# Every 16 MB of key and value loads, one 2 MB transfer issued as 112 partitions and two pieces of eight

## The chip, the cores and the metric

The kernel runs on one core of one Trainium2 chip. The metric is the device time of one execution in microseconds (us). Before the change the median of three runs was 1109.37 us (1105.71, 1109.37 and 1112.99).

## The reference, cut to what matters

One token for each of 8 batch rows passes through two identical layers. Each layer is an attention block over a cached sequence (16 query heads, 8 key/value heads, 4096 positions of 256 numbers) followed by an MLP block. Both layers read the same key cache and the same value cache.

```python
q = (x @ wq).reshape(B, Sq, Hq, Dh)                       # B=8, Sq=1, Hq=16, Dh=256
k = jnp.repeat(k_cache, 2, axis=1)                        # cache: 8 x 8 x 4096 x 256, bf16
scores = jnp.einsum("bhqd,bhkd->bhqk", q, k) * (Dh ** -0.5)
p = _softmax(scores, axis=-1)
o = jnp.einsum("bhqk,bhkd->bhqd", p, v)
...
x = x + _A_ref(_layernorm(x), A_k_cache, A_v_cache, A_wq, A_wo)    # attention
x = x + _B_ref(_layernorm(x), B_w1, B_w2, B_w3, B_w4)              # MLP
x = x + _A_ref(...)                                                # the same caches again
x = x + _B_ref(...)
```

Keys and values of one (batch row, head) are 2 MB each, so the two caches together hold 268 MB. All arithmetic hangs on streaming them through the core, once for each layer, less what is kept on the chip between the two.

## The kernel before, in words

**The cache buffer.** The tensor `kv` holds 30 slots ("quarters", `QUARTERS`) of 4 KB in each of the 128 partitions of SBUF. A (batch row, head) tile of K or V is viewed as 128 partitions of 16 KB of neighbouring positions and is cut along that row into four units of 4 KB per partition, 512 KB each; a unit takes one slot. K units are transposed by TensorE (`transpose_piece`, L1165), copied back over themselves by VectorE or ScalarE (`evacuate`, L1148 and L1149) and multiplied with the queries (L985); V units are used as they land (L1050). Some units of the first layer stay in their slots until the second layer has used them (`KEEP_K`, `KEEP_V`).

**The order of work.** The program is a list of operations with dependencies. `Plan.schedule` plays it through with assumed durations and writes down one fixed order for each engine. Loads go in program order on the SyncE queue (SP): `next_kv` (L191) waits in the plan until slots come free and merges up to four neighbouring units of one tile into one transfer of up to 2 MB (16 KB in each partition), and calls `issue_kv`. On the chip, a transfer that overwrites slots waits at SP for the instruction that used them last (a matmul of L985 or L1050); a consumer waits for the transfer's own semaphore, one for each slot (`slot_sem`), to reach the count that `issue_kv` has written into `o.dma`. `Plan.emit` (L446) turns this into waits and adds 16 to the semaphore with every transfer (L453 to L455).

**Weights.** `dma_once` and `dma` (L596 to L606) load each weight once, on the same queue. Two of them are loaded in halves that cover 64 partitions each: `wqx_sb` (L1236, 256 KB each) near the start, and `w3x_sb` (L1244, 112 KB each) later in the first batch row. The input `x_row` comes as two small transfers of eight rows; the output leaves in two transfers (L1193), the first of six rows of 896 bytes, the second of two.

**Batch rows.** Layer 1 of a row and layer 2 of the row before alternate; in each row there is a long stretch in which 2 MB transfers follow one another, and a shorter one around the MLP block in which loads are cut into 512 KB and 1 MB, because slots come free one at a time.

Of the kernel before, what the change touches and what calls it, by code (L numbers as in the profile page):

```python
# [6 lines left out]
P = 128  # L7
# [13 lines left out]
KEEP_K = 5  # L21
KEEP_V = 6
HOLD = 2
MARGIN4, MARGIN2 = 6, 2
REP = 24
AT = (-4, -3, -2)
# [433 lines left out]
def bass_interleave_layers__gqa_block_cached__mixer_s_mlp__decode_kernel(  # L460
# [119 lines left out]
    slot_sem = [nc.alloc_semaphore(f"s_slot{i}") for i in range(QUARTERS)]  # L580
    slot_n = [0] * QUARTERS
# [24 lines left out]
                4 * at - 0.5, *row)  # L606

    loads = [0]

    def issue_kv(o, n, q):  # L610

        (cache, b, h), u = o.unit.tile, o.unit.u
        src = cache[b, h].rearrange("(m s) d -> m (s d)", m=P)[:, u * 2048:(u + n) * 2048]
        dst = kv[:, q * 2048:(q + n) * 2048]
        slot_n[q] += 1
        o.emit = lambda eng: eng.dma_start(dst, src)  # L616
        o.dma = (slot_sem[q], 16 * slot_n[q])
        o.dur = ((n << 15) / 26.88e3 + 8 * 0.008) / FASTER

# [318 lines left out]

    KEPT_K[HKV - 1] = range(4 - HOLD)
    KEPT_V = {HKV - 1 - i: range(max(4 * i + 4 - KEEP_V, 0), 4) for i in range((KEEP_V + 3) // 4)}  # L940
    done = {}

    def front(layer, b, h, prio=None):
# [21 lines left out]
        for u in banks_of:  # L965

            ks[u] = ks[u + HOLD - 4]
            back_in[u + HOLD - 4] = u
        held = {}
# [462 lines left out]
```

## Time and profile before

| | |
|---|---|
| median of three runs | 1109.37 us |
| span of the profiled execution | 1109.5 us |
| TensorE busy | 971.3 us (88%) |
| VectorE, ScalarE, GpSimd busy | 573.0, 288.1, 97.9 us |
| bytes moved by DMA | 441.13 MB in 54099 packets |
| the SyncE queue's packets, share of 16 DMA engines | 96.9% |
| instruction fetch (queue 8) | 153 packets, 2.51 MB, 0.9% |
| transfers of 2 MB | 72 of K, 55 of V |
| chain of work that ended last | TensorE 54%, DMA 32%, SyncE queue 4% |

The profiled execution's own time is its span, 1109.5 us, 0.1 us from the median of the runs. A transfer is spread over 16 DMA engines; its packets are what the engines move one after another. "Share" counts the time that packets took as a share of 16 engines over the span, and where packets overlap by a few ns it comes out a little over 1. Windows below are in us from the start of the span.

### The profile page before, as it was taken

What the parts mean: (1) busy time and instruction counts of PE and PEld (TensorE: products, weight loads), DVE (VectorE), ACT (ScalarE), POOL (GpSimd) and SP (SyncE); (2) the same over time, 40 slices, a digit from 0 to 9 for tenths busy, and PEclk for the clock granted to TensorE, in tenths of its full rate; (3) what the DMA queues carried; (4) which work ended last, traced back from release to release, by engine and by line L of the source; (5) the groups of instructions that cost most, each with busy time, mean ns of one, the idle gap of its engine ahead of it and who ended that gap; (6) DMA issues with size and microseconds to landing.
All of it is one profiled execution on the core that took longest, in us unless ns stands there. A gap on an engine that the chain in (4) does not pass through costs nothing.

```text
span 1109.5 us, 42648 instructions
## 1 busy us (share of the span) xinstructions
PE 971.3 (88%) x19517; PEld 777.4 (70%) x19517; DVE 573.0 (52%) x1782; ACT 288.1 (26%) x844; POOL 97.9 (9%) x275
## 2 busy tenths in 40 slices
PE   4889889898889887999888898898889998899987
PEld 4678657786668756786667776777557886587774
DVE  4345445555455543655555554565445655366544
ACT  1133113331224301242122321234113330243120
POOL 0000010100100101010000100101010010101010
PEclk9899989989999969999898898999899997899898
DMA  9999999999999999999999989999999999999993
GB/s 332 410 424 421 389 388 424 425 421 380 412 424 424 418 344 428 422 425 418 378 424 423 421 326 381 425 424 420 387 402 424 425 410 364 420 423 407 329 399 163
DMA packets 54099, 441.13 MB, mean 398 GB/s; under 512 B 5776, under 2 KB 8992, under 8 KB 26528
## 3 DMA queue, kind: packets, MB, share of 16 engines
q1 hardware_dynamic: 53920, 438.41, 96.9%
q8 instruction: 153, 2.51, 0.9%
q14 instruction: 26, 0.21, 0.0%
HBM read 438.38 MB, written 0.01 MB: 395 GB/s over the span
## 4 chain that ended last, share of the span: by engine, by line
PE 54%; DMA 32%; SPq 4%; issue 4%; DVE 4%; ACT 1%; POOL 0%
PE psT L1165 20%; DMA kv<-in_A_k_cache_dram 20%; PE psM L985 15%; DMA kv<-in_A_v_cache_dram 12%; PE psP L1050 8%; SPq L616 4%; PE psR L1099 3%; PE psM L814 2%; PE psM L927 1%; PE psM L930 1%; DMA w3x_sb<-in_B_w_dram 1%; PE psP L1373 1%; PE psP L1074 1%; DVE oS L1066 1%; ACT pT L1019 1%
## 5 line engine op out<-in xcount | busy, mean ns | idle before, releaser
L1165 PE MATMUL psT<-ident_f,kv 128*128 128x128 f32 x2816 | 390.2, 284 | 23.3 <-DMA kv<-in_A_k_cache_dram 21.3
L1148 DVE COPY kv<-psT 128x512 f32<-128x512 f32 x415 | 284.3, 690 | 177.5 <-PE psT L1165 171.7
L1165 PEld LDWEIGHTS psT<-ident_f,kv 128*128 128x128 f32 x2816 | 313.2, 144 | 49.0 <-DMA kv<-in_A_k_cache_dram 28.3
L1149 ACT COPY kv<-psT 128x512 f32<-128x512 f32 x321 | 186.8, 586 | 385.4 <-PE psT L1165 384.9
L1050 PE MATMUL psP<-kv,pT 128*2 128x256 bf16 x4096 | 186.9, 292 | 27.8 <-issue 13.2
L985 PEld LDWEIGHTS psM<-q2T,kv 128*128 128x128 bf16 x4096 | 127.3, 99 | 48.0 <-issue 35.1
L985 PE MATMUL psM<-q2T,kv 128*128 128x48 bf16 x4096 | 142.5, 188 | 18.2 <-issue 14.4
L985 PEld LDWEIGHTS psM<-q1T,kv 128*128 128x128 bf16 x4096 | 135.1, 97 | 18.9 <-issue 12.5
L985 PE MATMUL psM<-q1T,kv 128*128 128x48 bf16 x4096 | 143.9, 184 | 2.2 <-issue 1.2
L1050 PEld LDWEIGHTS psP<-kv,pT 128*2 128x2 bf16 x4096 | 78.5, 84 | 70.2 <-issue 25.3
L1019 ACT ACTIVATE pT<-sS,nb,fac 128x32 bf16<-128x32 f32 x128 | 52.7, 417 | 244.0 <-DVE nb L1013 244.0
L1009 POOL PARTITION_ALL_REDUCE gm<-pm x128 | 45.6, 356 | 763.1 <-DVE pm L1007 718.0
L1004 DVE COPY sS<-psM 128x64 f32<-128x64 f32 x128 | 28.6, 223 | 108.4 <-PE psM L985 105.6
L1064 DVE CAST oS<-psP 128x256 bf16<-128x256 f32 x128 | 54.0, 422 | 49.3 <-PE psP L1050 46.9
L1099 PE MATMUL psR<-wo_sb,oT 128*1 128x448 bf16 x448 | 68.6, 390 | 4.2 <-DVE oT L1080 2.3
L1023 POOL PARTITION_ALL_REDUCE Db<-rs x128 | 51.1, 399 | 213.2 <-ACT pT L1019 213.2
L1074 PE MATMUL psP<-sel,oS 128*128 128x2 bf16 x512 | 32.1, 166 | 34.6 <-DVE oS L1066 31.1
L1074 PEld LDWEIGHTS psP<-sel,oS 128*128 128x128 bf16 x512 | 25.2, 99 | 52.5 <-DVE oS L1066 43.8
L1019 ACT ACTIVATE pT<-sS,nb 128x32 bf16<-128x32 f32 x128 | 40.9, 326 | 69.6 <-DVE nb L1013 69.5
L1066 DVE TENSOR_TENSOR oS<-psP,oS 128x256 bf16<-128x256 f32 x128 | 54.1, 423 | 3.5
L814 PEld LDWEIGHTS psM<-x2c,wq_sb 128*128 128x128 bf16 x768 | 30.5, 98 | 19.4 <-issue 6.9
L814 PE MATMUL psM<-x2c,wq_sb 128*128 128x24 bf16 x768 | 36.4, 184 | 6.2 <-issue 5.3
(157 smaller groups left out, 579.1 us busy)
## 6 DMA issues: line engine op xcount, KB each, us to landing
kv<-in_A_k_cache_dram SPq DMA_DIRECT2D x72, 2048.0 KB, 20.5
kv<-in_A_v_cache_dram SPq DMA_DIRECT2D x55, 2048.0 KB, 17.2
kv<-in_A_v_cache_dram SPq DMA_DIRECT2D x121, 512.0 KB, 7.5
kv<-in_A_v_cache_dram SPq DMA_DIRECT2D x54, 1024.0 KB, 10.6
kv<-in_A_k_cache_dram SPq DMA_DIRECT2D x23, 1024.0 KB, 12.6
kv<-in_A_v_cache_dram SPq DMA_DIRECT2D x5, 1536.0 KB, 10.9
kv<-in_A_k_cache_dram SPq DMA_DIRECT2D x12, 512.0 KB, 8.1
wo_sb<-in_A_wo_dram SPq DMA_DIRECT2D x1, 3584.0 KB, 45.4
```

The costliest lines, as they stand in the source:

```text
L814: last = t.matmul(bank[:, at + i * step:at + i * step + copies], w, r, start=(kc == 0), stop=(kc == 3))
L985: last = t.matmul(ps[:, SB + 2 * i:SB + 2 * i + 2 * REP], a[:, c:256:2], bcast(rhs(c), REP, 1), start=(c == 0), stop=(c == 1))
L1019: return a.activation(pT[nr][:, :, :].rearrange("p i j -> p j i")[:, jj, :], sview[:, jj, :], ACT.Exp, bias=nb[nm][:, jj:jj + 1], scale=sc ...
L1023: plan.op("pool", lambda gp: gp.partition_all_reduce(Db[nr][:, :], rs[nr][:, :], P, RO.add), 0.5, "sum", rd=[("rs", nr, 0), ("rs", nr, 1)] ...
L1050: last = t.matmul(ps[g4:g4 + 2, PV0:PV0 + DH], pT[nr][:, i, :], slot_ap(q, s * 256, 256), start=(i < 4), stop=(i >= 28), skip_group_check= ...
L1064: plan.op("dve", lambda v: v.tensor_copy(oS[:, 0, :], po), 0.36, "o", rd=[("pv", par, x) for x in range(4)], wr=["oS0"], banks=[bk], prio=hi)
L1066: plan.op("dve", lambda v: v.tensor_tensor(oS[:, 1, :], po, oS[:, 0, :], ALU.subtract), 0.36, "o", rd=["oS0"] + [("pv", par, x) for x in r ...
L1074: last = t.matmul(ps[:, PV1 + 2 * c:PV1 + 2 * c + 2], oS[:, w, c:DH:2], sel[:, :], start=(w == 0), stop=(w == 1))
L1099: last = t.matmul(psR[r:r + 1, 0:D], oT[no][:, i % 2, i // 2:i // 2 + 1], wo_sb[:, a:a + D], start=(k == 1 and i < 2), stop=(k == HKV - 1 ...
L1148: return e.tensor_copy(dst, psT[bank][:, :])
L1149: return e.copy(dst, psT[bank][:, :])
L1165: last = t.transpose(psT[bank][:, s * P:(s + 1) * P], src, ident_f[:, :])
```

## The change

`issue_kv` counts the units that it has issued. Whenever 32 units (16 MB) or more have gone out since the last time and the transfer at hand has four units (2 MB), this transfer is issued as three: one of the first 112 partitions and two of eight partitions each (112 to 119, 120 to 127). All three add 16 to the same slot's semaphore, and the count that consumers wait for grows by 48 instead of 16. The plan is computed with the same assumed duration, so the order on every engine stays as it was; the SyncE queue gets two more DMA instructions behind each such transfer. There are 21 of them, 9 of K and 12 of V.

```diff
+SPLIT, EVERY = 8, 32
...
     loads = [0]
+    since = [0]
 
     def issue_kv(o, n, q):
 
         (cache, b, h), u = o.unit.tile, o.unit.u
         src = cache[b, h].rearrange("(m s) d -> m (s d)", m=P)[:, u * 2048:(u + n) * 2048]
         dst = kv[:, q * 2048:(q + n) * 2048]
-        slot_n[q] += 1
-        o.emit = lambda eng: eng.dma_start(dst, src)
+        since[0] += n
+        top = P
+        if n == 4 and since[0] >= EVERY:
+            since[0] = 0
+            top = P - 16
+        slot_n[q] += 1 + (P - top) // SPLIT
+
+        def go(eng):
+            last = eng.dma_start(dst[0:top, :], src[0:top, :])
+            for p in range(top, P, SPLIT):
+                last.then_inc(slot_sem[q], 16)
+                last = eng.dma_start(dst[p:p + SPLIT, :], src[p:p + SPLIT, :])
+            return last
+        o.emit = go
         o.dma = (slot_sem[q], 16 * slot_n[q])
         o.dur = ((n << 15) / 26.88e3 + 8 * 0.008) / FASTER
```

## The prediction

> **What bounds the kernel now.** I read the page's first lines and its DMA rows, then the windows over single stretches, then the waits of SP. The page first:
>
> ```profile
> span 1109.5 us, 42648 instructions
> ...
> DMA  9999999999999999999999989999999999999993
> ...
> DMA packets 54099, 441.13 MB, mean 398 GB/s; under 512 B 5776, under 2 KB 8992, under 8 KB 26528
> ...
> q1 hardware_dynamic: 53920, 438.41, 96.9%
> q8 instruction: 153, 2.51, 0.9%
> ...
> kv<-in_A_k_cache_dram SPq DMA_DIRECT2D x72, 2048.0 KB, 20.5
> kv<-in_A_v_cache_dram SPq DMA_DIRECT2D x55, 2048.0 KB, 17.2
> ```
>
> The 16 DMA engines are at work for 96.9% of the span for SP's queue alone. A 2 MB transfer needs 2.097 MB / 423 GB/s = 4.96 us, but lands 20.5 us after its issue, so about four stand in line. The windows (us, PE, PEld, DVE, ACT, POOL busy, PE clock, DMA share, GB/s) tell long stretches from others:
>
> ```profile
> 20.60:26.60 6.00, 5.23 (x42) 4.14 (x39) 3.29 (x5) 2.93 (x5) 0.00 (x0) 1.00 1.05 272
> 30.00:40.00 10.00, 8.97 (x203) 7.42 (x202) 3.21 (x13) 2.37 (x10) 1.53 (x4) 0.83 1.00 422
> ...
> 114.00:122.00 8.00, 6.50 (x108) 4.08 (x103) 4.31 (x11) 1.31 (x5) 0.75 (x2) 1.00 1.06 353
> ...
> 145.00:245.00 100.00, 89.13 (x1708) 73.00 (x1705) 51.27 (x140) 29.44 (x86) 9.81 (x26) 0.93 1.01 420
> ...
> 385.00:415.00 30.00, 25.76 (x536) 16.09 (x536) 13.45 (x62) 1.98 (x10) 1.11 (x3) 0.72 0.95 351
> ...
> 550.00:635.00 85.00, 73.43 (x1417) 61.28 (x1415) 43.98 (x120) 24.27 (x73) 8.70 (x23) 0.92 1.01 425
> ```
>
> In the long stretches (145 to 245, 550 to 635) the engines are never idle and move 420 to 425 GB/s, while PE has 11% and 14% to spare: what a DMA engine loses there, the span loses. In the short ones (385 to 415) the share falls to 0.95. The first and third rows show something else: full engines (1.05, 1.06) that move only 272 and 353 GB/s. These are where the two transfers of `wqx_sb`, and later the two of `w3x_sb`, land, each covering 64 partitions:
>
> ```profile
> L599 SPq DMA_DIRECT2D wqx_sb<-in_A_wq_dram x2: 555/584/614, 4.2 to 4.8; - x2
> ...
> DMA to landing us min/median/max: 21.1/21.4/21.8
> ```
>
> (issued at 4.2 and 4.8 us, landed at 25.3 to 26.6).
>
> SP itself is no bound; it waits for PE to free slots:
>
> ```profile
> SPq L616 <- PE psM L985: 468.7, 86, 26.2
> SPq L616 <- PE psP L1050: 374.0, 151, 16.5
> ```
>
> **The change part by part.**
>
> *SP.* 21 transfers become three, 42 DMA instructions more. One takes 0.33 us at SP, 14 us in all, 0.65 us at a time. Queued behind them is the next transfer, for which PE waits only some 20 us later; SP waited 843 us in the two rows above. Cost 0; without four transfers in line it would be 14 us. The signals of the pieces are packets of 4 bytes, 9 ns each: 2 x 21 x 9 ns = 0.4 us, neglected.
>
> *How the rows fall.* The page counts 5776 packets under 512 B. That is 16 signals for each of 359 transfers (5744), 8 + 8 for the two of `x_row`, 6 + 2 for the outputs, and 8 data packets of 128 B. So 64 partitions still use 16 engines, and eight rows use eight, as the change says. A 16 KB row takes 4.96 / 8 = 0.62 us on its engine (0.614 in the packet records). A split gives eight engines 7 + 1 + 1 = 9 rows and the others 7: plus and minus 0.614 us, over 21 splits 12.9 us either way.
>
> *What it could balance.* In the packet records, the instruction fetches come in turn on the same eight engines: each takes 1.02 to 1.10 us, and the 16 KB packet behind it 1.08 to 1.16 instead of 0.614, so one costs some 1.55 us of its engine. 153 / 8 = 19 for each: 29.6 us more on these eight than on the others, 1.41 us between two splits, against the 1.23 us that a split shifts between the halves. If the fetching engines were all outside the pieces' eight, the change would even them out. I followed engines back to back (a packet starts 3 to 4 ns before the one ahead of it ends) from the six 896 B packets of the first output: five of these six engines never fetch, one does. If a transfer of six and one of eight start from the same engine, the pieces' eight hold at least one fetching engine, which then gets later: +12.9 us instead of -12.9. [...]
>
> *Transfers that cover fewer than 128 partitions.* This is the main term. The trace has no such transfer of 112 or of eight partitions among traffic; the nearest are those of 64.
> - Lowest price, by transfer: the window of `wqx_sb` lost (1 - 272/422) x 6 us = 2.13 us for two, that of `w3x_sb` (1 - 353/422) x 8 = 1.31 us for two, so 0.65 to 1.07 us each. Three at 0.65, plus the 0.61 us row: 2.6 us a split.
> - By packet: beside `wqx_sb`, 16 KB packets took some 1.13 us (1.08 to 1.18 mostly) instead of 0.614, and its own 4 KB packets 0.29 instead of 0.159. A transfer of 112 rows with 7 such packets on an engine loses 7 x 0.52 = 3.6 us, the two pieces cost 2 x 1.13 - 0.61 = 1.65 us: 5.3 us a split.
> - Highest: the slowest 16 KB packet in the records, 2.32 us, in the first microseconds of traffic, for the pieces (2 x 2.32 - 0.61 = 4.0), and 1.18 for the 112 rows (7 x 0.57 = 4.0): 8.0 us.
> - From below: the 896 B packets of `x_row`, eight partitions on an empty queue, mostly took 0.039 us, as elsewhere. Then there is no price at all, and the rows' -12.9 to +12.9 us remain.
>
> I take the price by packet, since the split's packets are of the size whose slowing was seen: 5.3 us. Eighteen of the 21 are issued in long stretches or at their edge; three (at 648, 778 and 1057 us of the old order) fall in short ones, where engines wait for slots, and are left out; without that cover they cost 16 us more. 18 x 5.3 = 95 us.
>
> [...]
>
> *What is late next.* Eight engines fall behind at every split; each transfer counts as landed when its last engine is done, so L1165 and L1050 wait, slots come free later, and the other eight engines run dry.
>
> *Sum.* 1109.5 + 95 = 1205 us. The 1109.5 are the profiled execution's own span; the median of the runs is 0.1 us lower.
>
> **Rivals.**
> - *Balance* (not slower): no price for fewer partitions, and all fetching engines outside the pieces' eight. At best -12.9 us, 1097; if the short stretches even out half of the lag anyway, 1103. For it: 1.41 us against 1.23 us. Against it: the two slow windows, and the one output engine that fetches.
> - *Wrong half*: no price, but one fetching engine or more among the eight: 1109.5 + 12.9 = 1122. For it: that engine; against it, the slow windows.
> - *Hidden*: the line of four transfers lets engines differ by several us, and the short stretches bring them together again: 1109.5. For it: share 0.95 there. Against it: 1.01 in the long ones, with no slack at the end of them.
> - That the pieces use all 16 engines, and nothing is shifted, is excluded by the 5776 small packets.
>
> **How the numbers follow.** A change of 1% (11 us) is about what a measurement of this kernel can tell from none; its three runs span 0.7%. The forecast has 0.72, balance 0.09, wrong half 0.08, hidden 0.11. The forecast's own range goes from 18 x 2.6 = 47 (1156) to 21 x 8.0 = 168 (1278). To hold 8 in 10 it reaches down over hidden, to 1106, and up to 1280; balance and the outermost of the forecast stay outside. Faster by over 1%: half of balance, 0.05. Within 1%: hidden, the other half, and a little of wrong half, 0.17. Slower: 0.78.
>
> **What would show it.** Small packets rise by 21 x 16 to 6112. In long windows the share stays at 1.0 or falls a little while the rate drops: a split for every 20.9 MB, 49.4 us before, takes 54.7, so 420 becomes some 380 GB/s. Waits of L1165 and L1050 for DMA grow, PE's busy time stays near 971 us. If the long windows still show 420 GB/s or more, the price is wrong, and the span then says which half fetches: below 1109, the others; above, the pieces' own.

## The result, and the profile after

The changed kernel takes 1288.74 us (median of four runs, 1280.30 to 1289.97) against 1111.18 us for the kernel before, run beside it: a ratio of 1.1599, 95% interval 1.1558 to 1.1639. The profiled execution's own span is 1286.2 us. The forecast was 1205 us, with a range from 1106 to 1280; the loss is 177.6 us where 95 were forecast. Over 21 splits it is 8.5 us each.

The page of the kernel after:

```profile
span 1286.2 us, 42690 instructions
...
PE 1025.5 (80%) x19517; PEld 812.3 (63%) x19517; DVE 574.5 (45%) x1782; ACT 287.8 (22%) x844; POOL 97.6 (8%) x275
...
DMA  9999999999999989999899998999999999999994
GB/s 347 372 348 320 375 314 402 334 307 342 347 403 327 366 250 334 398 299 380 263 341 413 320 358 273 344 416 329 345 349 323 371 339 366 410 329 418 339 319 191
DMA packets 54435, 441.13 MB, mean 343 GB/s; under 512 B 6112, under 2 KB 9328, under 8 KB 26864
...
q1 hardware_dynamic: 54256, 438.41, 96.6%
...
kv<-in_A_k_cache_dram SPq DMA_DIRECT2D x63, 2048.0 KB, 25.5
kv<-in_A_v_cache_dram SPq DMA_DIRECT2D x43, 2048.0 KB, 25.5
```

The engines are as busy as before (96.6% against 96.9%) and move the same bytes, but at 343 GB/s instead of 398. Busy share alone would show nothing wrong: a slow packet counts as busy. The small packets are 6112, as forecast (21 x 16 more): the split does what it says.

Windows of the kernel after (us, busy time of PE, PEld, DVE, ACT and POOL, PE clock, DMA share, GB/s), the first three around one split:

```profile
190.00:220.00 30.00, 27.89 (x490) 21.81 (x488) 15.11 (x40) 8.41 (x22) 2.26 (x6) 0.89 1.01 425
220.00:240.00 20.00, 12.17 (x162) 10.35 (x163) 7.08 (x18) 2.66 (x7) 0.75 (x2) 0.83 1.00 238
240.00:270.00 30.00, 27.60 (x487) 24.98 (x484) 17.70 (x44) 11.64 (x35) 3.77 (x10) 0.94 1.02 421
340.00:440.00 100.00, 81.02 (x1452) 68.36 (x1450) 47.13 (x122) 29.32 (x80) 8.28 (x22) 0.91 1.01 365
```

Between splits the old rate of 420 to 425 GB/s is back. Around the split, for 20 us, full engines (1.00) move 238 GB/s: (1 - 238/423) x 20 = 8.7 us are lost, the 8.5 us a split of the whole. TensorE runs dry in that time (12.2 of 20 us).

The waits of the kernel after (engine, line, releaser: us in total, times, longest):

```profile
PEld psP L1064 <- DMA kv<-in_A_v_cache_dram: 74.3, 36, 6.1
PE psP L1064 <- DMA kv<-in_A_v_cache_dram: 69.9, 27, 6.0
PEld psT L1179 <- DMA kv<-in_A_k_cache_dram: 63.4, 33, 6.1
PE psT L1179 <- DMA kv<-in_A_k_cache_dram: 54.4, 26, 5.9
...
SPq L625 <- PE psM L999: 522.9, 85, 37.8
SPq L625 <- PE psP L1064: 451.9, 151, 21.2
```

The same waits of TensorE before (lines moved down by 14 at TensorE, and by nine at SP):

```profile
PEld psT L1165 <- DMA kv<-in_A_k_cache_dram: 28.3, 23, 4.7
...
PEld psP L1050 <- DMA kv<-in_A_v_cache_dram: 22.3, 33, 1.6
...
PE psT L1165 <- DMA kv<-in_A_k_cache_dram: 21.3, 18, 4.4
...
PE psP L1050 <- DMA kv<-in_A_v_cache_dram: 12.3, 22, 1.4
```

TensorE now waits for keys and values, and SP waits longer for TensorE to free the slots (522.9 and 451.9 us in its two rows, against 468.7 and 374.0).

The packet records say which packets are slow. Of the 16256 packets of 16 KB, 235 took over 0.7 us before and 4006 after, and these slow packets have a median of 1.16 us and a mean of 1.20 in place of 0.614. What all of SP's packets took beyond the median of their size came to 35.2 us on each of 16 engines before and 201.5 us after: 166 us more, near the 177 us that the kernel takes longer.

### The profile page after: what moved, and what is told of

Same layout as the page of the kernel before. It is cut to its first block, busy times and chain, and to the rows that moved or that the text cites. A ratio compares the mean times of both kernels' runs of the same rounds, so it can differ in the third digit from the quotient of the medians.

```text
span 1286.2 us, 42690 instructions
## 1 busy us (share of the span) xinstructions
PE 1025.5 (80%) x19517; PEld 812.3 (63%) x19517; DVE 574.5 (45%) x1782; ACT 287.8 (22%) x844; POOL 97.6 (8%) x275
## 2 busy tenths in 40 slices
DMA packets 54435, 441.13 MB, mean 343 GB/s; under 512 B 6112, under 2 KB 9328, under 8 KB 26864
## 3 DMA queue, kind: packets, MB, share of 16 engines
q1 hardware_dynamic: 54256, 438.41, 96.6%
## 4 chain that ended last, share of the span: by engine, by line
PE 49%; DMA 41%; issue 5%; DVE 3%; SPq 1%; ACT 1%; POOL 0%
DMA kv<-in_A_k_cache_dram 27%; PE psT L1179 16%; PE psM L999 13%; DMA kv<-in_A_v_cache_dram 11%; PE psP L1064 8%; PE psR L1113 3%; PE psM L828 2%; DMA wqx_sb<-in_A_wq_dram 2%; DMA w3x_sb<-in_B_w_dram 2%; PE psM L941 1%; PE psP L1387 1%; PE psM L844 1%; PE psM L944 1%; PE psP L1088 1%; DVE oS L1080 1%
## 5 line engine op out<-in xcount | busy, mean ns | idle before, releaser
L1179 PE MATMUL psT<-ident_f,kv 128*128 128x128 f32 x2816 | 414.4, 295 | 64.4 <-DMA kv<-in_A_k_cache_dram 54.4
L1179 PEld LDWEIGHTS psT<-ident_f,kv 128*128 128x128 f32 x2816 | 333.0, 151 | 94.1 <-DMA kv<-in_A_k_cache_dram 63.4
L1064 PE MATMUL psP<-kv,pT 128*2 128x256 bf16 x4096 | 197.5, 307 | 93.3 <-DMA kv<-in_A_v_cache_dram 69.9
L999 PE MATMUL psM<-q2T,kv 128*128 128x48 bf16 x4096 | 145.7, 189 | 28.9 <-issue 25.8
L999 PEld LDWEIGHTS psM<-q2T,kv 128*128 128x128 bf16 x4096 | 130.2, 100 | 56.9 <-issue 44.8
L999 PEld LDWEIGHTS psM<-q1T,kv 128*128 128x128 bf16 x4096 | 139.5, 99 | 23.5 <-issue 17.0
L999 PE MATMUL psM<-q1T,kv 128*128 128x48 bf16 x4096 | 148.3, 186 | 2.6 <-issue 1.6
L1113 PE MATMUL psR<-wo_sb,oT 128*1 128x448 bf16 x448 | 72.1, 405 | 7.9 <-DMA wo_sb<-in_A_wo_dram 4.0
L1033 ACT ACTIVATE pT<-sS,nb 128x32 bf16<-128x32 f32 x128 | 40.8, 326 | 97.0 <-DVE nb L1027 96.9
```

Of the source, the lines that this page charges most:

```text
L999: last = t.matmul(ps[:, SB + 2 * i:SB + 2 * i + 2 * REP], a[:, c:256:2], bcast(rhs(c), REP, 1), start=(c == 0), stop=(c == 1))
L1033: return a.activation(pT[nr][:, :, :].rearrange("p i j -> p j i")[:, jj, :], sview[:, jj, :], ACT.Exp, bias=nb[nm][:, jj:jj + 1], scale=sc ...
L1064: last = t.matmul(ps[g4:g4 + 2, PV0:PV0 + DH], pT[nr][:, i, :], slot_ap(q, s * 256, 256), start=(i < 4), stop=(i >= 28), skip_group_check= ...
L1113: last = t.matmul(psR[r:r + 1, 0:D], oT[no][:, i % 2, i // 2:i // 2 + 1], wo_sb[:, a:a + D], start=(k == 1 and i < 2), stop=(k == HKV - 1 ...
L1179: last = t.transpose(psT[bank][:, s * P:(s + 1) * P], src, ident_f[:, :])
```

## The experiments

All kernels keep the order of the kernel after and, but for the run with half as many splits, its 21 split points; they change only the list of transfers (destination, source) in `issue_kv`. Each transfer of a split signals as in the change. "A split" is (ratio - 1) x 1111 us / 21. Three theories stand in the expectations. *Count*: what costs is that there are more transfers, signals and instructions. *Pieces*: each transfer of few partitions costs by itself. *Places*: engines get slow where their rows meet other engines' rows at the same part of the partitions.

**Three transfers of all partitions.** The 16 KB are cut by columns instead of rows.

```diff
+            parts = [(dst[:, a:b], src[:, a:b]) for a, b in ((0, 7168), (7168, 7680), (7680, 8192))]
```

> The same 21 transfers go as three, but cut along the row: 14 KB, 1 KB and 1 KB in all 128 partitions. Three theories. Count (three transfers, their signals and SP's work cost the time): all of it stays, +150 to +180 us over before. Pieces (the eight-row pieces cost): nothing is left, within 5 us of before. Places (engines write into partitions that other engines' rows lie beside, which holds for any transfer of fewer than 128 partitions): nothing is left, within 5 us of before.

1115.35 us, ratio 1.0022 (0.9996 to 1.0049). 42 more instructions at SP, and more signals, cost nothing that can be measured. *Count* falls.

**One half of the change at a time.** First only the 112 rows (the last 16 partitions keep what was in the slot), then 112 and 16 rows in two transfers.

```diff
+            parts = [(dst[0:112, :], src[0:112, :])]
```

> Only the 112-partition transfer is issued; partitions 112 to 127 of these 21 transfers are left out and keep what their slots held. Without any price each engine has 7 rows instead of 8: -13 us. Count: -13 us, as one transfer stays one. Pieces: -13 to +10 us. Places: 16 engines with 7 rows each no longer match the rows' places, so half of the price or more stays, +60 to +110 us.

1218.70 us, ratio 1.0975 (1.0918 to 1.1032): 108 us, and 13 more, since an eighth of the bytes of 21 transfers is left out. So 112 rows cost 121 / 21 = 5.8 us each, before any piece is there.

```diff
+            parts = [(dst[0:112, :], src[0:112, :]), (dst[112:128, :], src[112:128, :])]
```

> 112 partitions, and one piece of 16 that uses 16 engines with one row each. Count: two transfers instead of three, about half, +80 us. Pieces of eight: gone, within 15 us of before. Places: +100 to +150 us, somewhat under the changed kernel's +177.

1258.38 us, 1.1332 (1.1253 to 1.1411): 7.0 us a split. With the two pieces it is 8.5. By my count of rows (7 + 1 for each engine) nothing is uneven here, yet most of the loss is there.

**Two halves, lower and upper.**

```diff
+            parts = [(dst[0:64, :], src[0:64, :]), (dst[64:128, :], src[64:128, :])]
```

> Partitions 0 to 63 and 64 to 127, 16 engines with four rows each, as the two slow weight loads of the kernel before. Count: +80 us (two transfers). Pieces: within 10 us of before. Places: each half is written at half speed, 9.6 us instead of 4.9, so +80 to +110 us.

1275.82 us, 1.1489 (1.1427 to 1.1551): 165 us, 7.9 us a split, against the 80 to 110 us expected. The half speed expected of each half was an estimate; in the trace before, 16 KB packets beside `wqx_sb` took some 1.13 us instead of 0.614. The two transfers of `wqx_sb`, on which my prices rested, have this shape and cost 2.13 us together.

**Four pieces,** once as neighbouring rows, once four apart on the chip, once four apart in memory. The last two put rows in other places than the reference has them.

```diff
+            parts = [(dst[a:b, :], src[a:b, :]) for a, b in ((0, 96), (96, 104), (104, 112), (112, 120), (120, 128))]
...
+            parts = [(dst[0:96, :], src[0:96, :])] + [(dst[96 + j:P:4, :], src[96 + 8 * j:104 + 8 * j, :]) for j in range(4)]
...
+            parts = [(dst[0:96, :], src[0:96, :])] + [(dst[96 + 8 * j:104 + 8 * j, :], src[96 + j:P:4, :]) for j in range(4)]
```

> Partitions 0 to 95 (six rows on each of 16 engines) and four pieces of eight neighbouring partitions. Base for the next two. Places: about as the changed kernel or somewhat more, +160 to +200 us over before; if only the transfer with most rows counted, +90 to +110.

> As e5, but each piece writes eight partitions that lie four apart (96, 100, ... 124, then 97, 101, ...), while it reads the same eight neighbouring rows of the cache as in e5; so rows of these 32 partitions land in other partitions than they should. Only the place in SBUF differs. Places on the chip: each of the pieces' engines then writes to a place of its own, and 30 to 60 us of e5's time go. Places in HBM (it is the order of reading that slows): as e5, within 10 us.

> The mirror of e6: each piece reads rows that lie four apart in the cache and writes eight neighbouring partitions, as e5 does. Places on the chip: as e5, within 10 us. Places in HBM: 30 to 60 us less than e5.

In order: 1.2058 (1.196 to 1.2156), 1.1898 (1.1725 to 1.2072) and 1.2036 (1.1977 to 1.2095); 10.9, 10.0 and 10.8 us a split. How rows are read in memory makes no difference that can be seen (1.2036 against 1.2058). On the chip, four apart gained 18 us where *Places* expected 30 to 60, and the intervals overlap, so these runs can't tell it from nothing. That theory looked weak at this point; the last two runs suggest why this was the wrong test: all these rows lie in the upper half. That rows four apart have places of their own, here and in the 16 pieces below, was assumed; no run shows it.

**Half as many splits.** `EVERY = 64` leaves 11 of 21.

> The changed kernel with a split every 32 MB: 11 instead of 21. If every split costs the same and none is hidden, +177 x 11/21 = +93 us over before. If engines that have got out of step make the next split dearer: less than +80. If short stretches hide some: more than +105 or less than +80, by where the 11 fall.

1197.25 us, 1.0748 (1.069 to 1.0806): 83 us, 7.6 us for each of 11. That is a little under the 93 us of equal splits: about linear in their number.

**Even and odd partitions.** The sizes, counts and signals of the two halves, with other partitions.

```diff
+            parts = [(dst[j:P:2, :], src[j:P:2, :]) for j in range(2)]
```

> In place of a split, two transfers of 64 partitions: the even ones and the odd ones, instead of the lower and the upper half. Half-transfer packets, sizes and counts are those of the lower and upper halves, which cost 163 us over before (7.8 us a split). [...] Rows per engine (what matters is that a transfer of fewer than 128 partitions is dealt out to the engines in another order than the 128-partition traffic around it): the price stays, 150 to 220 us over before.

1110.61 us, ratio 0.9992 (0.9969 to 1.0015). The price is gone altogether, where *Rows per engine* had 150 to 220 us: 165 us hang on which 64 partitions a transfer has. The window of this kernel's long stretch, with splits in it, and the same stretch of the kernel with two halves:

```profile
150.00:240.00 90.00, 79.90 (x1510) 65.26 (x1503) 46.02 (x127) 25.79 (x76) 9.07 (x24) 0.91 1.01 424
```

```profile
150.00:240.00 90.00, 69.36 (x1347) 52.33 (x1346) 36.17 (x118) 15.76 (x48) 6.02 (x16) 0.87 1.00 345
```

424 against 345 GB/s at nearly the same share (1.01 and 1.00). Packets of 16 KB over 0.7 us are 234 here (235 before), 3942 with halves. This is the run that decides for *Places*: a transfer of 64 partitions has no price by itself. It says nothing yet of pieces of eight rows.

**Less of the row.** The split covers only the last 4 KB of each partition; then two kernels in which the last 2 KB go as 16 pieces of eight, neighbours or four apart.

```diff
+            parts = [(dst[:, 0:6144], src[:, 0:6144])] + [(dst[a:b, 6144:], src[a:b, 6144:]) for a, b in ((0, 112), (112, 120), (120, 128))]
...
+            parts = [(dst[:, 0:7168], src[:, 0:7168])] + [(dst[a:a + 8, 7168:], src[a:a + 8, 7168:]) for a in range(0, P, 8)]
...
+            parts = [(dst[:, 0:7168], src[:, 0:7168])] + [(dst[a + j:a + 32:4, 7168:], src[a + j:a + 32:4, 7168:]) for a in range(0, P, 32) for j in range(4)]
```

> The split covers only the last 4 KB of each partition's 16 KB: one transfer of 128 partitions and 12 KB, then 112 + 8 + 8 partitions of 4 KB. A price by the bytes that go as fewer than 128 partitions: a quarter of 177 us, 44 us over before, about 2 us a split. A price by transfer (a fixed disturbance whenever one with fewer partitions comes by): 177 us. Balance would shift a quarter of 12.9 us, 3 us, not to be seen.

1167.40 us, 1.0499 (1.0441 to 1.0558): 55 us, near a quarter of 177 (44) and far from 177. Mostly a price by bytes.

> In place of a split: one transfer of 128 partitions and 14 KB of each, then the last 2 KB as 16 transfers of eight neighbouring partitions each, which cover all 128 between them. An eighth of the bytes. By bytes at the price of pieces (the 16 rows as 8 + 8 beside one transfer of 16 cost 31 us more, four pieces 51 us more than two): 20 to 50 us over before. By transfer: 16 pieces at some 1.2 us (51 us over 21 splits over two pieces more) each, 400 us.

> As the run with 16 pieces of eight neighbouring partitions, with each piece's eight partitions four apart, each row on its own place. Places: half of that run's price, 10 to 25 us over before. No part of the places in it: the same as that run within 8 us.

1.0513 (1.0477 to 1.0548) and 1.0465 (1.0428 to 1.0503): 57 and 52 us. Both are above what was expected, and 5 us apart where *Places* said half. In both, half of the pieces lie in the upper half.

**The change's rows, spread out.** Does place also make up the price of 112 + 8 + 8? A ladder of rows spread over all partitions, each (a, s) a transfer of every s-th row from a:

```diff
+            parts = [(dst[a:P:s, :], src[a:P:s, :]) for a, s in ((0, 2), (1, 4), (3, 8), (7, 16), (15, 16))]
```

> The change's 112 + 8 + 8 rows with all of them spread over the partitions: every second (64 rows), every fourth from 1 (32), every eighth from 3 (16), together 112, and two pieces of eight, every sixteenth from 7 and from 15. The same nine rows for eight engines and seven for the others. If a price comes only from rows that crowd into a part of the partitions, it is nearly gone: the uneven rows alone are left, 12.9 us more or less than before (1099 or 1124) by whether the eight engines of the pieces fetch instructions, or 0 when the line hides it. If every transfer of few rows costs by itself (pieces at some 1.2 us each, as four neighbouring pieces against two showed), 50 us or more over before.

> As the run with 64 + 32 + 16 + 8 + 8 rows, but the last 16 rows in one transfer (every eighth from 7): 64 + 32 + 16 + 16, eight rows for every engine. No unevenness: if rows spread out have no price, as before within 5 us, and the difference of the two runs is what uneven rows do (-13, 0 or +13 us). If transfers of 16 rows have a price of their own, 20 to 50 us over before.

> Every second row (64), every fourth from 1 (32), every fourth from 3 (32). These reach all places evenly, two rows for each engine in the small ones: as before within 5 us. If the number of rows has a price of its own besides their place, some 10 us over before.

> 64 + 32 rows spread out, the last 32 as four pieces of eight, every sixteenth row from 3, 11, 7 and 15: ten rows for eight engines and six for the others, twice the change's unevenness. Uneven rows alone: +26 us if the pieces' eight engines are the ones that fetch, -13 to 0 (more than levelled out) if the others are. If each piece costs by itself, 25 us or more above the run with two pieces.

| transfers of a split | ratio (95%) | us a split | 16 KB packets over 0.7 us |
|---|---|---|---|
| 64 + 32 + 32 | 1.0013 (0.9995 to 1.0032) | 0.1 | 243 |
| 64 + 32 + 16 + 16 | 1.0551 (1.0521 to 1.0580) | 2.9 | 2001 |
| 64 + 32 + 16 + 8 + 8 | 1.0634 (1.0589 to 1.0680) | 3.4 | 1960 |
| 64 + 32 + four pieces of 8 | 1.0864 (1.0827 to 1.0901) | 4.6 | 2281 |
| 112 + 8 + 8, neighbouring rows (the change) | 1.1599 (1.1558 to 1.1639) | 8.5 | 4006 |

Rows every two and every four are free here (0.1 us a split). Every eight (16 rows) they are not (2.9 us), although by my count each engine has its one row: the ladder was meant to take all of the price away and took 60% of it, so the expected 1099 or 1124 us for the spread split was wrong (1186.57). The level run tells only that uneven rows are not the larger part: 0.4 us a split between it and the one with two pieces. Two pieces more cost 26 us more, which was expected both of uneven rows and of a price by piece; that run doesn't tell them apart.

**The same pieces in the lower and in the upper half.** 64 + 32 rows as above, and two pieces of eight rows four apart. 16 rows are left out in each.

```diff
+            parts = [(dst[a:b:s, :], src[a:b:s, :]) for a, b, s in ((0, P, 2), (1, P, 4), (3, 32, 4), (35, 64, 4))]
...
+            parts = [(dst[a:b:s, :], src[a:b:s, :]) for a, b, s in ((0, P, 2), (1, P, 4), (67, 96, 4), (99, 128, 4))]
```

> Every second row (64), every fourth from 1 (32), and two pieces of eight rows four apart in the lower half: 3 to 31 and 35 to 63. The 16 rows 67, 71 ... 127 are left out, so the output is not the reference's. Eight engines move 8 rows, the others 6. [...] If small transfers cost by themselves: 30 to 60 us over before.

> The mirror of the run with the pieces in the lower half: the two pieces of eight are rows 67 to 95 and 99 to 127, and 3, 7 ... 63 are left out (the output is not the reference's). Sizes, counts and engines are the same. [...] By small transfers alone: the same as that run within 8 us.

Lower: 1105.97 us, 0.9953 (0.9926 to 0.9980). Upper: 1160.44 us, 1.0435 (1.0401 to 1.0470). The two kernels differ in nothing but the 64 that is added to 16 row numbers, and are 54 us apart. Windows around a split, lower and then upper:

```profile
205.00:210.00 5.00, 5.00 (x103) 4.95 (x100) 3.22 (x8) 1.95 (x4) 0.34 (x1) 1.00 0.99 419
210.00:215.00 5.00, 5.00 (x95) 4.97 (x91) 3.35 (x8) 2.71 (x9) 0.50 (x3) 1.00 1.00 419
```

```profile
205.00:210.00 5.00, 4.00 (x71) 3.85 (x68) 2.54 (x5) 1.17 (x2) 0.00 (x0) 1.00 1.09 324
210.00:215.00 5.00, 2.02 (x31) 1.90 (x29) 1.09 (x2) 0.58 (x1) 0.00 (x0) 0.96 0.94 282
```

324 and 282 GB/s for 5 us each are 1.17 + 1.67 = 2.8 us lost, near the 2.3 us a split of the ratio. In the lower half these windows show no trace of the split. Of the 16 KB packets, 302 took over 0.7 us in the lower run and 1633 in the upper one (235 before). The rows that are left out would have taken 13 us at 423 GB/s; with them, the pieces cost 0.4 us a split in the lower half and 2.9 in the upper. So a piece of eight rows costs little by itself here; nearly all of its price depends on where its rows lie. Why the upper half is the dear one was not shown: no run tells which engine moves which row.

## Why the prediction was right and wrong

- *Direction: right; mechanism: right for these transfers, too wide as it was put.* The three transfers of a split slow the packets; small packets are 6112; the share stayed near 1.0 while the rate fell; the four DMA waits of TensorE grew two to six times. But the main term spoke of transfers that cover fewer than 128 partitions, and 64 even ones, or 32 four apart, cost nothing (0.9992, 1.0013): what counts is which partitions they are. SP's work cost nothing (cut by columns, ratio 1.0022).
- *The step that failed: "7 such packets on an engine loses 7 x 0.52 = 3.6 us, the two pieces cost 2 x 1.13 - 0.61 = 1.65 us: 5.3 us a split".* The price of a packet was nearly right: a slow one took 1.20 us on average (median 1.16) against 1.13 in the sum. The count was not. I charged only the split's own packets, 128 a split. There are 3771 more slow packets of 16 KB after than before, 180 a split, so at least 52 a split belong to full transfers ahead and behind; smaller packets are slower too (8 KB: 345 ns on average, 318 before; 4 KB: 184, 178 before). On each engine these 52 make 52 x 0.58 / 16 = 1.9 us a split, and the packets of other sizes another 1.2 us (26 us in all). In the sum's own terms: the 112 rows measured 5.8 us (by the run that has only them) instead of 3.6, and the pieces 8.5 - 5.8 = 2.7 instead of 1.65.
- *The number of splits.* The sum counted 18, on the ground that three lie in short stretches. All 21 at 5.3 us would have been 111 us. No run measured what those three cost in time. The packet records of the kernel after speak against free ones: these three are followed, up to the next split, by 127, 123 and 123 slow packets of 16 KB, and all 21 by 123 or more (before, some 11 on average in a 21st of the span); and the window of a split in a long stretch lost 8.7 us against 8.5 on average.
- *The lowest price,* from the `wqx_sb` and `w3x_sb` windows, was farthest off, because I took it by transfer. The two of `wqx_sb` lost 2.13 us for 512 KB; by bytes that is 2.13 x 4 = 8.5 us for 2 MB, and the two halves of 2 MB measured 7.9. (The two of `w3x_sb`, 1.31 us for 224 KB, would give 12 us, so bytes are no exact measure.) The run that splits only the last 4 KB (2.6 us a split) says too that the price goes by bytes. My bound of 8.0 us a split, built on the slowest packet seen, was just too low, and with it the range.
- *Rate and period.* "Some 380 GB/s" was 365 in the window above, and the 49.4 us between splits become, with the measured price, 49.4 + 8.5 = 57.9 instead of 54.7.
- *PE busy near 971: wrong.* It is 1025.5 us, with a mean granted clock of 0.867 instead of 0.930, and the matmul of L1179 took 295 ns on average (L1165 before: 284). That can explain little of the loss, since slow packets alone come to 166 us and TensorE is busy only 80% of the longer span; why the clock falls was not tried.
- *The balance rivals.* That both pieces of a split fall to the same eight engines, nine rows there and seven on the others, was assumed; no run shows it. The change can't show what uneven rows do behind 177 us. The run with pieces in the lower half could: by the same assumption its eight engines move 8 rows and the others 6, and it gains 5.2 us (2.2 to 8.2) with 5.5 MB less to move, 13 us at 423 GB/s. Relief for the other eight alone was worth up to 26 us (2 x 0.614 us x 21, an estimate) had these been all the fetching ones. A price of the pieces themselves could hide some of that gain. The small gain speaks for the engine of the first output that fetches, as in the rival *Wrong half*, but does not prove it. I found no complete kernel faster than the one before, and the even ones (even and odd, 64 + 32 + 32) are the same as it.

That engines meet, as *Places* has it, and at what, was not shown: no run tells which engine moves which row. What the runs show is the pattern: 64 even and 64 odd rows, and 32 rows four apart, cost nothing (0.9992, 1.0013); two halves cost 7.9 us a split, two transfers of 16 rows eight apart 2.9, the first 112 rows alone 5.8, and two pieces of eight rows four apart 2.9 in the upper half and 0.4 in the lower.

## What to carry to other kernels

When transfers to the whole buffer run back to back, judge any other transfer by the partitions that it covers: here rows spread evenly over all 128 (every second, every fourth) cost nothing (0.9992, 1.0013), while the change's blocks of neighbours (8.5 us a split) and the two halves (7.9) slowed the full transfers around them as well: 180 and 177 more slow packets of 16 KB a split, where the split itself has 128. Shifting bytes between engines made no complete kernel here faster. A DMA share near 1.0 says nothing about this (1.00 at 238 GB/s, 1.01 at 425); read the GB/s beside it, in windows of a few us. And when a price is taken from a rare row of the trace, scale it by bytes and by what lies beside it before it becomes a bound: here nearly the right price of a packet, with too small a count of packets, was off by 1.6 times.

## What I had not expected

- One 2 MB transfer cut into 112 + 8 + 8 rows nearly halves the rate of all 16 engines for some 20 us (238 instead of 423 GB/s), although alone it is 5 us of work.
- The same 64 + 64 rows cost 7.9 us a split as halves and nothing as even and odd.
- Adding 64 to 16 row numbers of otherwise equal transfers is worth 2.6 us a split (54 us in all).
- TensorE's granted clock was lower (0.867 against 0.930) in a kernel in which it waits more.
